# A two-layer attention and MLP kernel on one Trainium2 core: the ramp's loads, score units, bank pairs and query transposes rearranged

## Chip, core and metric

The kernel runs on one core of one Trainium2 chip. The metric is the device time of one launch in microseconds (us). Engines are named as in the profile: PE (TensorE matmul), PEld (its weight load), DVE (VectorE), ACT (ScalarE), POOL (GpSimd), SP (SyncE, which issues DMAs).

## What is computed

A sequence of 2048 tokens of width 576 in bfloat16 passes twice through the same attention block and the same MLP. The inputs `B_x` and the weights are shared by both layers.

```python
def _A_ref(x, wqkv, wo):                    # H = 32 heads, Dh = 18, window W = 256
    qkv = (x @ wqkv).reshape(B, S, 3, H, Dh).transpose(2, 0, 3, 1, 4)
    q, k, v = qkv[0], qkv[1], qkv[2]
    scores = jnp.einsum("bhqd,bhkd->bhqk", q, k) * (Dh ** -0.5)
    mask = (idx[:, None] - idx[None, :] >= 0) & (idx[:, None] - idx[None, :] < W)
    p = softmax(where(mask, scores, -1e9))
    return einsum("bhqk,bhkd->bhqd", p, v).transpose(0, 2, 1, 3).reshape(B, S, D) @ wo
def _B_ref(x, w1, b1, w2, b2):              # F = 4608
    h = gelu(layernorm(x) @ w1 + b1)
    return h @ w2 + b2
x = A_x
for _ in range(2):
    x = x + _A_ref(layernorm(x), A_wqkv, A_wo)
    x = x + _B_ref(layernorm(x), B_w1, B_b1, B_w2, B_b2)
```

## The kernel before

**Tiles and stages.** The tokens are 16 tiles of 128. Four tiles make a chunk, so each layer has four chunks and there are eight in all (`CH`); chunk 0 is the first of layer 1 and chunk 4 the first of layer 2. For each chunk the stages are: layer norm (`ln1`, `ln1_in`), projections q, k, v (`qkv`), scores and exponentials and PV per group of four heads (`E`, `E0`; 8 groups), the output projection with the second layer norm (`tail`), and the MLP in three parts of 12 of its 36 column tiles, first half `G_part` (W1 and gelu), second half `mm2` (W2). The attention of one chunk is laid beside the MLP of the chunk before it, so that ACT's exponentials stand beside PE's MLP matmuls. Chunks 0 and 1 have no earlier MLP to stand beside; the time until the first MLP matmul is called the ramp here.

**How the order is made.** Each operation is a task with a cost, a latency and a priority in `Plan.add`. `Plan.schedule` (line 263) runs a list scheduler over a model of the engines: it takes the task that can start first, ties go by priority, and it gives out the eight PSUM banks with `place` (line 273). The priorities are shifted by a table `PL.nudge`, one number per stage. The resulting order is written out per engine with semaphore waits (`Sched`), and the chip keeps that order on each engine. SP issues all DMAs in one such order; a task on SP that waits holds back all that stand behind it. Where PE would idle in the first 140 us of the plan, filler matmuls are put in (`keep_warm`, `warm_fn`, profile line L683).

**Banks.** Score units take two pairs of banks out of `SC = (0, 2, 4)`, that is banks 0-1, 2-3 or 4-5. Projections, transposes and the MLP's second half take a bank of `FILL`, PV one of `OUT`, both (7, 6, 5, 4). `place` takes among the possible banks the one that has been free longest.

**Start.** SP issues the loads of x tile 0, x tile 1, wq, x tiles 2 and 3, wk, wv (each weight as one large piece and two small ones, `w_load`), then x tiles 4 to 7. The layer norm's statistics are DVE work (L696, L700), the variance step (L709) and the power (L711) POOL work, the normalised tile DVE work (L721). For chunk 0 the normalised tile is transposed on PE (L738) and copied by ACT (L741); later tiles are transposed by DMA (L744). ACT's first instruction is the load of its table for the exponential (L1138).

**Projections.** `qkv` makes q, k and v of a tile with 10 matmuls each (L800 in chunk 0, L781 or L784 in chunk 1, L840 from chunk 2 on). ACT and DVE copy the results (L858, L861, v: L848). k of chunk 0 is transposed on PE (L874) and copied by ACT (L878); q of chunk 0, and all q and k after it, by a DMA transpose from SP (L880).

**Scores.** A score unit is one PE task (L909) of 3 or 4 blocks of 128 query columns for four heads, two exponentials on ACT (L918, 128x768 or 128x1024), and masks on POOL for the blocks at the window's edges (L939). One PV task per group follows (L956), then four DVE steps (L967 to L977). A unit holds one of six slots of the tile `pT` until its PV is done. In the first chunk of a layer there are no keys before it, and each group has three units of 3 blocks: with `(key tile, first query tile, number of query tiles, column)`

```python
if t0 == 0:
    us = [[(0, 0, 3, 0)], [(1, 1, 3, 128)], [(2, 2, 2, 256), (3, 3, 1, 128)]]
```

**Loads in the ramp.** A load may be gated by a name that it reads: wo by `aq0` (chunk 0's first group finished), the first W1 slab by `k3`, the next by `v0h0` and `aq2`, b1 and b2 by `k3`, x tiles 8 to 11 by `v1h0`, tiles 12 to 15 by `xm0_3`, the first W2 third by `aq5` and `aq7`. `xm0_i` is the transposed MLP input of tile i of chunk 0, `xa_i` that of the projections.

Of the kernel before, what the change touches and what calls it, by code (L numbers as in the profile page):

```python
# [9 lines left out]
P = 128  # L10
# [176 lines left out]
class Plan:  # L187
# [75 lines left out]
    def schedule(self):  # L263
# [9 lines left out]
        def place(t):  # L273
# [27 lines left out]
        def starves(t, st, got):  # L301
# [4 lines left out]
            where, when = place(f)  # L306
# [12 lines left out]
        served = {}  # L319
        n = len(self.tasks)  # L320
        while len(order) < n:
            best = None
            cands = []
            for e in ENGS:
                for t in released[e]:
# [4 lines left out]
                    if t.alloc:  # L330
                        got, when = place(t)
# [33 lines left out]
            if t.dma is not None:  # L365
# [15 lines left out]
                done = at + t.move  # L381
                for o in served:
                    if o != t.eng and served[o] > at:
                        both = min(t.move, served[o] - at)
# [3 lines left out]
                q.append((done - t.move, done, t.desc))  # L388
# [42 lines left out]
SWITCH = 0.095  # L431
TURN_FROM = 40.0
# [4 lines left out]
def build_kernel(nc, A_x, A_wqkv, A_wo, B_x, B_w1, B_b1, B_w2, B_b2, out):  # L437
# [19 lines left out]
    PVG = [()] * 8  # L457
# [22 lines left out]
    PL.nudge = {"": -230.72, "b": 275.87, "ea0.0": 68.12, "ea0.2": -36.73, "ea0.p0": 25.27, "ea0.p1": 8.39, "ea0.p2": 19.16,  # L480
# [403 lines left out]
    def units_of(k):  # L884
# [6 lines left out]
        if t0 == 0:  # L891
            us = [[(0, 0, 3, 0)], [(1, 1, 3, 128)], [(2, 2, 2, 256), (3, 3, 1, 128)]]
# [423 lines left out]
```

## Time and profile before

| what | us |
|---|---|
| median of 3 runs (865.04 to 865.78) | 865.6 |
| the profiled execution | 864.13 |
| its span, first to last instruction | 862.3 |
| first projection matmul (L800) begins | 7.56 |
| first MLP matmul (L1076) begins | 87.07 |
| last matmul ends | 859.41 |
| busy time of DVE, ACT, POOL | 392.0, 593.2, 377.9 |

In a line of the timeline, the first number is the start in us from the span's start, the second the length, then engine, line, operation, tile written and tile read with their shapes, and how many instructions are merged in the line; in brackets stands the engine's idle time before it and what ended it. In a line of the groups, the shapes are followed by the count, the busy time and the mean length of one in ns, and the idle time before them. Matmuls overlap in the engine, so the mean length of one is more than what it adds; what it adds is the busy time divided by the count, or the distance to the next instruction.

### The profile page before, as it was taken

The page shows a single profiled execution, that of the slowest core. Times are in us where ns is not written, and L with a number is a line of the kernel's source. Part 1 is how long each engine was busy: PE and PEld are TensorE (multiplying, and loading weights), DVE is VectorE, ACT ScalarE, POOL GpSimd, SP SyncE. Part 2 cuts the span into 40 slices and gives each one's busy share as a digit, 9 for nine tenths or more (in the row PEclk, how much of TensorE's full clock was granted, in tenths as well). Part 3 has the DMA queues.
Part 4 walks back from the last instruction along what each step waited for, and adds up shares of the span by engine and source line. Part 5 has one row for each costly group of instructions (what it writes and reads, how often), then busy time and mean ns, then how long its engine had stood idle before and what let it go on. Part 6 is the DMA issues. An engine that isn't in the chain of part 4 may idle for free.

```text
span 862.3 us, 26990 instructions
## 1 busy us (share of the span) xinstructions
PE 848.7 (98%) x11578; PEld 520.5 (60%) x11578; DVE 392.0 (45%) x934; ACT 593.2 (69%) x741; POOL 377.9 (44%) x560
## 2 busy tenths in 40 slices
PE   8899999999999999999999999999999999999998
PEld 6556556656556565565655655656556656656656
DVE  7689424655228542384424832655224434243012
ACT  4796788768667588573875876737787589771730
POOL 4687544465135653264421863425454276222100
PEclk9999999999999999999999999999999999999999
DMA  7887435351583615957359443673536953355320
GB/s 192 197 193 142 124 125 148 109 163 44 166 181 107 163 43 166 204 93 169 90 151 218 92 139 125 116 177 98 173 112 119 289 155 105 126 166 146 120 83 28
DMA packets 181862, 119.77 MB, mean 139 GB/s; under 512 B 107440, under 2 KB 181744, under 8 KB 181744
## 3 DMA queue, kind: packets, MB, share of 16 engines
q1 hardware_dynamic: 181744, 118.05, 53.7%
q8 instruction: 91, 1.49, 0.7%
q14 instruction: 27, 0.22, 0.1%
HBM read 90.10 MB, written 2.36 MB: 107 GB/s over the span
## 4 chain that ended last, share of the span: by engine, by line
PE 87%; DMA 4%; DVE 4%; ACT 2%; issue 2%; SPq 1%; POOL 1%; POOLq 0%; DVEq 0%; ACTq 0%
PE ps L1076 31%; PE ps L781 27%; PE ps L784 9%; PE ps L840 8%; PE ps L909 6%; PE ps L956 4%; ACT pT L918 2%; DMA xnTm<-xn 2%; PE ps L800 1%; DMA xnTa<-xn 1%; DVE x_res L1019 1%; DVE xn L721 1%; DVE st_all L696 1%; SPq L633 1%; DMA wqkv<-in_A_wqkv_dram 1%
## 5 line engine op out<-in xcount | busy, mean ns | idle before, releaser
L939 POOL TENSOR_SCALAR_AFFINE_SELECT pT<-pT 128x512 bf16<-128x512 bf16 (+1 forms) x368 | 282.8, 789 | 250.1 <-ACT pT L918 244.9
L918 ACT ACTIVATE pT<-ps 128x1024 bf16<-128x1024 f32 (+1 forms) x384 | 345.1, 974 | 58.0 <-PE ps L909 57.6
L1076 PE MATMUL ps<-xnTm,w_sb 64*128 64x512 bf16 x2592 | 290.5, 376 | 0.9 <-DVE x_res L1019 0.3
L1086 ACT ACTIVATE hT<-ps,b1col 128x512 bf16<-128x512 f32 x276 | 167.4, 687 | 173.9 <-PE ps L1076 173.4
L1076 PEld LDWEIGHTS ps<-xnTm,w_sb 64*128 64x128 bf16 x2592 | 128.8, 94 | 142.5 <-issue 6.4
L781 PE MATMUL ps<-w_sb,hT 128*128 128x288 bf16 x1506 | 201.1, 287 | 0.0
L1019 DVE TENSOR_TENSOR x_res<-ps,x_res 128x288 f32<-128x288 f32 x224 | 100.0, 450 | 188.2 <-PE ps L781 162.1
L781 PEld LDWEIGHTS ps<-w_sb,hT 128*128 128x128 bf16 x1506 | 139.9, 98 | 51.5 <-issue 15.6
L840 PE MATMUL ps<-wqkv,xnTa 64*128 64x288 bf16 x1296 | 91.7, 283 | 1.6 <-DVE x_res L1019 1.1
L967 DVE STREAM_TRANSPOSE oq<-ps 128x512 f32<-128x512 f32 x64 | 45.8, 716 | 98.9 <-PE ps L956 98.0
L784 PE MATMUL ps<-w_sb,hT 128*32 128x288 bf16 x2424 | 83.7, 287 | 0.1
L861 DVE CAST qn<-ps 128x288 bf16<-128x288 f32 x120 | 49.0, 450 | 76.4 <-PE ps L840 68.8
L840 PEld LDWEIGHTS ps<-wqkv,xnTa 64*128 64x128 bf16 x1296 | 61.3, 94 | 31.4 <-issue 2.7
L784 PEld LDWEIGHTS ps<-w_sb,hT 128*32 128x32 bf16 x2424 | 62.2, 97 | 13.6 <-issue 4.2
L909 PE MATMUL ps<-qT,kT 32*128 32x384 bf16 (+2 forms) x1216 | 64.1, 276 | 2.8 <-ACT pT L918 2.3
L696 DVE BATCH_NORM_STATS2 st_all<-x_res 128x6 f32<-128x288 f32 (+1 forms) x128 | 53.4, 442 | 6.7 <-DMA x_res<-in_A_x_dram 5.8
L709 POOL TENSOR_SCALAR vtmp<-mv_all 128x1 f32<-128x1 f32 (+1 forms) x43 | 8.8, 204 | 107.7 <-DVE mv_all L700 105.3
L848 DVE CAST vA<-ps 128x288 bf16<-128x288 f32 x64 | 26.5, 450 | 63.2 <-PE ps L840 59.5
L1092 POOL TENSOR_TENSOR x_res<-x_res,b2bc 128x576 f32<-128x576 f32 x32 | 40.2, 1275 | 32.8 <-ACT hT L1086 32.8
L956 PE MATMUL ps<-pT,vA 128*20 128x384 bf16 (+2 forms) x1408 | 50.5, 276 | 0.2 <-DVE qn L861 0.2
L909 PEld LDWEIGHTS ps<-qT,kT 32*128 32x128 bf16 x1216 | 19.4, 92 | 42.8 <-issue 26.3
L781 PE MATMUL ps<-wo_sb,attT 128*128 128x288 bf16 x320 | 42.1, 287 | 0.3 <-DVE qn L861 0.3
(56 smaller groups left out, 465.1 us busy)
## 6 DMA issues: line engine op xcount, KB each, us to landing
w_sb<-in_B_w_dram SPq DMA_DIRECT2D x46, 864.0 KB, 6.0
w_sb<-in_B_w_dram SPq DMA_DIRECT2D x48, 768.0 KB, 4.7
w_sb<-in_B_w_dram SPq DMA_DIRECT2D x96, 48.0 KB, 4.4
wqkv<-in_A_wqkv_dram SPq DMA_DIRECT2D x3, 576.0 KB, 5.6
x_res<-in_A_x_dram SPq DMA_DIRECT2D x3, 576.0 KB, 5.7
wqkv<-in_B_w_dram SPq DMA_DIRECT2D x2, 864.0 KB, 6.3
out_dram<-x_res SPq DMA_DIRECT2D x12, 144.0 KB, 2.0
wo_sb<-in_A_wo_dram SPq DMA_DIRECT2D x4, 144.0 KB, 2.6
```

What stands on the lines that cost most here:

```text
L696: add("dve", lambda e, i=i, s=s: e.bn_stats(st_all[:, t, i, :], s[:, t, i * HB:(i + 1) * HB]), reads=res, writes=[f"st{t}_{i}"], cost=0.37 ...
L781: return e.matmul(bank(b)[:, 0:HB], lhs, rhs, start=start, stop=stop, skip_group_check=True)
L784: ins = e.matmul(bank(b)[32 * j:32 * j + 32, 0:HB], lhs[:, 32 * j:32 * j + 32], rhs, start=start, stop=stop, tile_position=(0, 32 * j), sk ...
L840: ins = e.matmul(bank(bs[o])[:, 0:HB], xnTa[r:r + 64, c, i * 128:(i + 1) * 128], wqkv[r:r + 64, c, col:col + HB], start=(c == 4), stop=(ph ...
L861: add("dve", lambda e, b=bs[o], dst=dst: e.tensor_copy(dst, heads_of(bank(b))), reads=[bs[o]], writes=[f"qn{sl}h{o}"], cost=0.375, lat=0.1 ...
L909: ins = e.matmul(two(bs[j // 2])[:, j % 2, col:col + nq * 128], k_of(T0 + so)[0][32 * j:32 * j + 32, g, :], qs[32 * j:32 * j + 32, g, qo * ...
L918: add("act", lambda e, h2=h2: e.activation(pT[:, sl, 2 * h2:2 * h2 + 2, lo:hi], two(bs[h2])[:, :, lo:hi], ACT.Exp, scale=SCALE), reads=[bs ...
L939: add("pool", lambda e, ap=ap, pat=pat, sgn=sgn, kind=kind: e.affine_select(ap, ap, pattern=pat, compare_op=(ALU.is_ge if kind == "d" else ...
L956: ins = e.matmul(bank(bo)[32 * j:32 * j + VW, qo * 128:(qo + nq) * 128], vA[:, (T0 + so) % VS, 8 * j + g, :], pT[:, sl, j, col:col + nq * ...
L1019: add("dve", lambda e: e.tensor_tensor(x_res[:, t, sl], bank(b)[:, 0:HB], x_old[:, t, sl], ALU.add), reads=[b] + ([f"xin{t}"] if first els ...
L1076: ins = e.matmul(bank(bks[i])[:, 0:n], w1_sb[r:r + 64, sls[i], col:col + 128], xnTm[r:r + 64, k % 2, c, 0:n], start=(c == 4), stop=(ph == ...
L1086: add("act", lambda e, ff=ff, hd=hd, bk=bk: e.activation(hd[:, 0:n], bank(bk)[:, 0:n], ACT.Gelu_apprx_tanh, bias=b1col[:, ff:ff + 1]), rea ...
```

## The change

- **Loads.** x tile 1 and x tiles 2 and 3 are issued from ACT's queue, behind the table load; SP goes from x tile 0 straight to wq, wk, wv. wo is gated by `aq2`; the three first W1 slabs by `aq3`, `aq5` and `xm0_0`; b1 and b2 by `aq5`; x tiles 8 to 11 by `xa2`, 12 to 15 by `aq2` of chunk 1; the first W2 third by `xm0_2` and `xm0_3`.
- **Score units.** In the first chunk of each layer the blocks of a unit may belong to several groups. For groups 0 to 2 of chunk 0 there are 8 units in place of 9; for the other sets of three groups 7 in place of 9, and for the set of two 5 in place of 6. The PV task takes each block from its unit; a slot is given back when the last of its groups is done.
- **Banks.** `SC` gains the pair 6-7. `place` takes the first listed bank of those that are free at the task's start; only where none is does the time count.
- **Queries.** q of tiles 1 and 2 of chunk 0 is transposed on PE, in two halves of four 128x128 transposes with a bank each; ACT copies the first half and DVE the second. q of tiles 0 and 3 stays with the DMA.
- **Layer norm of chunk 0.** The variance step goes from POOL to DVE. For tile 0 the 64 duplicated columns are computed by DVE from x (not copied by ACT), and the five transposes go to two banks, copied by ACT (3) and DVE (2).
- **The planner.** Several modelled costs and latencies of DMAs change, a DMA of 500 descriptors or more behind a transpose gets 0.8 us more (`TURN_DMA`), and the table `PL.nudge` is new throughout, so the order of the tasks is new everywhere.

The diff, cut to its core:

```diff
-                    key = (max(bank_free[b] for b in bs), n)
+                    key = (max(now, max(bank_free[b] for b in bs)), n)
...
-    PL.nudge = {"": -230.72, "b": 275.87, "ea0.0": 68.12, "ea0.2": -36.73, "ea0.p0": 25.27, "ea0.p1": 8.39, "ea0.p2": 19.16,
+    PL.nudge = {"": -0.78, "b": -26.43, "ea0.0": -39.17, "ea0.1": -14.18, "ea0.2": 0.51, "ea0.p0": 239.47, "ea0.p1": -20.24,
...
-    SC = (0, 2, 4)
+    SC = (0, 2, 4, 6)
...
     xin_load(0, 1)
-    xin_load(1, 1)
     w_load(0)
-    xin_load(2, 2)
     w_load(1)
     w_load(2)
+    table("exp", -10)
+    xin_load(1, 1, q="act", prio=-9)
+    xin_load(2, 2, q="act", prio=-8)
...
-        add("pool", lambda e: e.tensor_scalar(vtmp[:, t0:t0 + n], var, sc, bi, op0=ALU.mult, op1=ALU.add),
+        add("dve" if t0 < 4 and not fused else "pool", lambda e: e.tensor_scalar(vtmp[:, t0:t0 + n], var, sc, bi, op0=ALU.mult, op1=ALU.add),
...
+            bs = [Bank(FILL)] * 2 if i else [Bank(FILL), Bank(FILL)]
+            groups = ((0, 1, 2, 3), (4,)) if i else ((0, 1, 2), (3, 4))
...
-                if k == 0 and (w == "k"):
+                if k == 0 and (w == "k" or i in (1, 2)):
+                    n = 2 if w == "q" else 1
+                    for y in range(n):
+                        b = Bank(FILL)
+                        gg = range(y * G // n, (y + 1) * G // n)
...
+                        if y == 0:
+                            add("act", lambda e, dd=dd, src=src: e.copy(dd, src()), reads=[b], writes=[dn], cost=0.12 + 0.83 / n, lat=0.17, prio=prio)
+                        else:
+                            add("dve", lambda e, dd=dd, src=src: e.tensor_copy(dd, src()), reads=[b], writes=[dn + "d"], cost=0.5, lat=0.14, prio=prio)
                     continue
...
-        if t0 == 0:
-            us = [[(0, 0, 3, 0)], [(1, 1, 3, 128)], [(2, 2, 2, 256), (3, 3, 1, 128)]]
...
+        on = lambda g, *ps: [(g,) + p for p in ps]
+        if CH[k][1]:
+            seq = [on(g, *u) for g in gs for u in units_of(k)]
+        elif k == 0 and gs[0] == 0:
+            seq = [on(g, (0, 0, 3, 0)) for g in gs]
+            bs = [on(g, (1, 1, 3, 0), (2, 2, 1, 384)) for g in gs]
+            cs = [on(g, (2, 3, 1, 256 * n), (3, 3, 1, 256 * n + 128)) for g, n in ((0, 0), (1, 1), (2, 0))]
+            seq += [bs[0], cs[0] + cs[1], bs[1], bs[2], cs[2]]
+        else:
+            seq = []
+            for g in gs:
+                seq += [on(g, (0, 0, 3, 0), (2, 2, 1, 384)), on(g, (1, 1, 3, 0), (2, 3, 1, 384))]
+            seq.insert(2, [(g, 3, 3, 1, 128 * n) for n, g in enumerate(gs)])
...
-    xin_load(8, 4, ["v1h0"], -4)
+                xin_load(8, 4, ["xa2"], -4)
...
-                w1_load(-1, ["k3"])
+                w1_load(-1, ["xm0_0"])
-            w2_load(0, 1, ("aq5", "aq7"))
+            w2_load(0, 1, ("xm0_2", "xm0_3"))
...
-                w1_load(-1, ["v0h0"])
-                w1_load(-1, ["aq2"])
+                w1_load(-1, ["aq3"])
+                biases()
+                w1_load(-1, ["aq5"])
...
-                xin_load(12, 4, ["xm0_3"], 0)
+                xin_load(12, 4, ["aq2"], 3)
```

More of the change, by code (lines that the diff above doesn't have):

```diff
@@ L271, in schedule, with place @@
         bank_free = {b: 0.0 for b in range(self.nbanks)}
-        def place(t):
+        def place(t, now):
             got = []
@@ L305, in starves @@
             f = feed[fed]
-            where, when = place(f)
+            where, when = place(f, max(free["pe"], f.ready))
             if where is None:
@@ L801, in fn @@
                 return ins
-            add("pe", fn, reads=reads, writes=[bs[o]], cost=mm_cost(HB) * KD, lat=0.22, prio=prio, alloc=[bs[o]], after=after, mode=mode, wide=wide)
+            add("pe", fn, reads=reads[o] if isinstance(reads[0], list) else reads, writes=[bs[o]], cost=mm_cost(HB) * KD, lat=0.22, prio=prio, alloc=[bs[o]], after=after, mode=mode, wide=wide)
         return bs
@@ L906, in fn @@
             ins = None
-            for (so, qo, nq, col) in parts:
+            for (g, so, qo, nq, col) in tiles:
                 for j in range(4):
@@ L941, in scores, with pv @@
                 reads=[f"p{sl}h0", f"p{sl}h1"], writes=[f"p{sl}m{mi}"], cost=0.12 + 0.475 * nb, prio=prio)
-        return sl
-    def pv(k, g, units, bo, first, last, prio):
-        slots.extend(sl for _, sl in units)
+        return sl, users
+    def pv(k, g, units, prio):
+        bo = Bank(OUT)
+        for _, (sl, users) in units:
+            users.discard(g)
+            if not users:
+                slots.append(sl)
         l, t0, nt = CH[k]
@@ L949, in pv @@
         PL.part = f".p{g}"
+        todo = [(p[1:], sl) for parts, (sl, _) in units for p in parts if p[0] == g]
         def fn(e):
             ins = None
-            todo = [(p, sl) for parts, sl in units for p in parts]
             for n, ((so, qo, nq, col), sl) in enumerate(todo):
@@ L956, in fn @@
                     ins = e.matmul(bank(bo)[32 * j:32 * j + VW, qo * 128:(qo + nq) * 128], vA[:, (T0 + so) % VS, 8 * j + g, :],
-                                   pT[:, sl, j, col:col + nq * 128], start=(first and n == 0), stop=(last and n == len(todo) - 1),
+                                   pT[:, sl, j, col:col + nq * 128], start=(n == 0), stop=(n == len(todo) - 1),
                                    tile_position=(0, 32 * j), skip_group_check=True)
             return ins
-        rd = [f"p{sl}{x}" for _, sl in units for x in ("h0", "h1", "m0", "m1", "m2")]
-        rd += [f"v{(T0 + p[0]) % VS}h{o}" for parts, _ in units for p in parts for o in range(2)]
-        ncol = sum(p[2] for parts, _ in units for p in parts) * 128
+        rd = [f"p{sl}{x}" for _, (sl, _) in units for x in ("h0", "h1", "m0", "m1", "m2")]
+        rd += [f"v{(T0 + p[0]) % VS}h{o}" for p, _ in todo for o in range(2)]
+        ncol = sum(p[2] for p, _ in todo) * 128
         add("pe", fn, reads=rd, writes=[bo], cost=0.02 + ncol * 0.000425, prio=prio, lat=0.2, mode="c",
-            alloc=([bo] if first else ()))
-        if not last:
-            return
+            alloc=[bo])
         add("dve", lambda e: e.transpose(oq[:, 0:4 * nt, :].rearrange("p b c -> p (b c)"), bank(bo)[:, 0:nt * 128]),
@@ L992, in E @@
[L992 to L1009 removed]
+    def E(k, gs, prio):
+        gs = list(gs)
+        on = lambda g, *ps: [(g,) + p for p in ps]
[6 more added lines that the diff above has]
+            seq += [bs[0], cs[0] + cs[1], bs[1], bs[2], cs[2]]
+        else:
+            seq = []
+            for g in gs:
+                seq += [on(g, (0, 0, 3, 0), (2, 2, 1, 384)), on(g, (1, 1, 3, 0), (2, 3, 1, 384))]
+            seq.insert(2, [(g, 3, 3, 1, 128 * n) for n, g in enumerate(gs)])
+        at = {g: max(n for n, u in enumerate(seq) if any(p[0] == g for p in u)) for g in gs}
+        done = []
+        todo = list(gs)
+        for n, u in enumerate(seq):
+            done.append((u, scores(k, u, prio)))
+            while todo and at[todo[0]] + PVLAG <= n:
+                pv(k, todo[0], [x for x in done if any(p[0] == todo[0] for p in x[0])], prio - 0.1)
+                todo.pop(0)
+        for g in todo:
+            pv(k, g, [x for x in done if any(p[0] == g for p in x[0])], prio - 0.1)
@@ L1134, in mm2 @@
         PL.part = ""
-    def table(name, prio):
-        if name == "exp":
-            fn = lambda e: e.preload_act_table_set("exp_and_others")
-        else:
-            fn = lambda e: e.preload_act_table(ACT.Gelu_apprx_tanh)
-        add("act", fn, cost=1.4, lat=0.0, fifo="act", plain=True, prio=prio)
     def ln1(k, prio):
```

147 lines of the change are left out of this document (69 added, 78 removed), and 141 rows, old and new, of the table add.

## The prediction

> **What bounds the kernel now.** I read the busy times of the whole span first, then the same by stage, then TensorE's waits, and the timelines of the stage that loses most. The profiled execution took 864.13 us, with a span of 862.3, so 1.83 us lie around the span; the median shown is 865.6, 1.47 above this execution. Every saving below is worked out in the profiled execution and then taken off the median.
>
> ```profile
> PE 848.7 (98%) x11578; PEld 520.5 (60%) x11578; DVE 392.0 (45%) x934; ACT 593.2 (69%) x741; POOL 377.9 (44%) x560
> ```
>
> TensorE (PE) is the bound. The stage table gives, for each stretch, its length, the busy time of PE, weight load, VectorE (DVE), ScalarE (ACT) and GpSimd (POOL), then the granted clock, the DMA share and GB/s.
>
> ```profile
> 10.29:28.79 18.50, 18.32 (x173) 13.47 (x174) 13.16 (x39) 13.79 (x24) 7.53 (x15) 1.00 0.92 192
> 28.79:36.00 7.21, 4.49 (x81) 2.46 (x79) 3.92 (x14) 3.48 (x6) 4.73 (x7) 0.76 0.92 181
> 36.00:60.00 24.00, 22.58 (x360) 12.95 (x358) 19.64 (x46) 23.78 (x33) 19.00 (x28) 1.00 0.72 156
> 60.00:87.07 27.07, 25.94 (x402) 16.27 (x403) 25.14 (x62) 19.30 (x22) 20.00 (x34) 1.00 0.82 168
> 87.07:860.00 772.93, 770.07 (x10516) 470.23 (x10516) 324.11 (x759) 529.70 (x655) 321.00 (x458) 1.00 0.51 134
> ```
>
> From 87.07 on, PE idles 2.9 us in 773, with 0.6 of it after its last matmul: little can be won there except work. Before, PE idles 0.2, 2.7, 1.4 and 1.1 us in the four stages. The worst, 28.79 to 36, also has a granted clock of 0.76. PE's timeline of it:
>
> ```profile
> 29.46 0.35 PE L909 MATMUL ps<-qT,kT 32*128 32x256 bf16 x8 [0.38 <-DVE mv_all L700]
> 30.72 0.34 PE L909 MATMUL ps<-qT,kT 32*128 32x384 bf16 x4 [0.91 <-ACT pT L918]
> 32.48 2.59 PE L784 MATMUL ps<-wqkv,xnTa 128*32 128x288 bf16 x40 [1.42 <-DMA xnTa<-xn]
> ```
>
> PE waits 0.91 for an exponential and 1.42 for the transposed input of the second chunk. Then its 40 matmuls take 2.59 us; by the row of this form over the span (L784 on hT: 2424 in 83.7 us) they take 1.38, so 1.21 more is lost to the low clock behind the wait. The chain of waits shows what came late:
>
> ```profile
> 22.36 4.98 DMA qT<-qn
> 27.34 0.05 issue
> 27.39 0.31 PE ps L909
> 27.70 4.74 DMA xnTa<-xn
> 32.44 0.04 issue
> 32.48 2.59 PE ps L784 x40
> ```
>
> The transposes of q's fourth tile and of the second xnTa tile land 4.7 to 5.0 us after issue. The SyncE queue shows why they start late: weight and bias loads stand among them (19.41 w1, 19.89 input rows 8 to 11, 21.66 b1, 25.77 b2), and the first xnTa transpose goes out at 23.70, though the last copy it and its three fellows need (POOL L729) ended at 20.49. ACT pays as well:
>
> ```profile
> 29.85 2.92 ACT L918 ACTIVATE pT<-ps 128x768 bf16<-128x768 f32 x4 [0.56 <-PE ps L909]
> 35.95 23.16 ACT L918 ACTIVATE pT<-ps 128x768 bf16<-128x768 f32 x32 [3.18 <-PE ps L909]
> ```
>
> It idles 3.18 us and then runs 23.16 us without a gap, PE stopping for it in bits of 0.20 to 0.34.
>
> **The change part by part.**
>
> Start. PE's second group of L800 begins at 10.29, on the key weights, which land at 10.16. Their first piece is issued at 4.05 and would go out some 1.1 us earlier, with the loads of x1 and x2-3 (0.43 and 0.59 us of issue) gone to ACT, which idles to 5.55 except for its table load. But the DMA share is 0.8 to 1.0 from about 4 us on, and bytes decide: x0 to x3, wq and wk, 1.9 MB, come in any case. If all of them still come first, only the start of the stream moves, 0.43 or less; if the x loads came behind wk, 0.44 MB at the 350 GB/s of this stretch is 1.2 us; if they take half of wq's rate, wq lands up to 0.7 later than 7.5, which the 0.84 us of idle between q's first tile and 10.29 absorbs nearly. Bounds -1.2 and +0.7; I take -0.3, nearest the byte count. The Trainium skill (DMA: Bandwidth & Descriptors, Issuing engines are not separate DMA queues) says that DMAs started from several engines interleave on the same 16 DMA engines and that only issue time is saved; by that the -1.2 falls out. No DMA from ACT is in this trace.
>
> Moving the variance step to DVE and splitting xnTa0's copy over two banks shorten the chain of x0 by a few tenths (POOL L709 0.19 us). It is ready at 6.81 while wq comes at 7.5, so I cost both at nothing. If wq came first, they gain up to 0.5.
>
> q1 and q2 on PE. Two DMA transposes leave SyncE (1.24 us of issue each) and 16 transposes come to PE. L874's row: 8 have a mean of 219 ns, but the next matmul follows after 0.45 us, so 16 cost +0.9, on a PE that is 99% busy there. All in line at 219 ns it would be 3.5. The Trainium skill (TensorE: Matmul & The Clock Gate, Part 4: PE-mode transpose) gives about 275 ns in one kernel and says that the full clock does not engage for transposes; 16 would then cost 4.4 us and the sum below would be near zero. Here the rows show 56 ns from one to the next and a clock of 1.00. The copies, half on ACT (a whole one, L878, is 1.03, so about 1.1 us for two halves) and half on DVE (between the 0.45 of a cast and the 0.72 of L967 each), lie beside a PE-bound stage in which ACT idles 4.7 and DVE 5.3 us. Without that cover, 1.1 us of exponentials would be late.
>
> Later loads. w1, rows 8 to 11, b1 and b2 leave the stretch 19 to 32; SyncE keeps q0, q3 and the xnTa transposes. The first can go at about 20.5 instead of 23.70, four at 1.25 us, with q3's among them: second tile issued by about 24, landing by 29 even at 5 us, when PE gets through chunk 0's projections (28.3 plus 0.9). So the 1.42 wait and the 1.32 us of low clock (1.21, and 0.11 on the 16 matmuls of L956 behind it) go, and of the other 1.3 us I take 0.5: -3.2 in all, bounds 0 and -4.0. What is late next is POOL: the mask that releases the first PV ended at 32.53. The later homes have room: W1 is wanted at 87.07, the second W1 slab group at 117, w2 at 99.8; a w2 load gated by the last two transposes of chunk 0 (before 87) has over 10 us where it takes 5 to 6. If that cover were gone, PE would wait for w2 at once.
>
> Shared units. Chunk 0 has 24 score units of 384 columns and gets 20 (8, 7 and 5); the first chunk of layer 2 gets 19. Columns stay (72 blocks each). The two exponential forms price a unit:
>
> ```profile
> L918 ACT ACTIVATE pT<-ps 128x1024 bf16<-128x1024 f32 x288 | 273.9, 1027 | 42.3 <-PE ps L909 42.0
> L918 ACT ACTIVATE pT<-ps 128x768 bf16<-128x768 f32 x96 | 71.3, 816 | 15.7 <-PE ps L909 15.6
> ```
>
> 0.951 and 0.743 us of busy time each, 0.81 ns a column, so a fixed 0.12: 8 fewer save ACT 0.95 us in chunk 0. Of the 1.42 us that PE idles under that bound I take half: -0.7 (bounds 0, -1.4). On PE a unit of 384 columns takes 0.27 to the next instruction and one of 512 takes 0.33, so 0.09 is fixed: 4 and 5 units, less up to 0.01 for each piece that is cut in two, give -0.3 and -0.4. Masks cost POOL some 0.4 us more (18 singles of 0.62 for 12 and 3 doubles of 1.10), and POOL idles 5 us of those 24.
>
> 60 to 87, and all after. DVE is 93% busy there; I take 0, between -1.5 (PE's idle time with 0.39 of warm-up filler) and +1.5. The new order moves everything behind 87; the idle time in it is bits of 0.2 to 1.1, and I take 0, within 1.6 both ways. A fourth bank pair is for planned order only, and costs nothing by itself; it is costed with the second rival.
>
> Sum: -0.3 + 0.9 - 3.2 - 0.7 - 0.3 - 0.4 = -4.0, so 861.6.
>
> **Rivals.** First, DVE becomes the bound of 60 to 87: what is won before 60 is waited for there. For it speak the 25.14 of 27.07; against it DVE's 13 us of idle time between 20 and 87, and PV results that come earlier too. Left are -0.4 in layer 2 and some 0.6: 864.6.
>
> Second, slower: the planner now takes the first-listed bank of those free at that moment, no longer the one free longest, so a PSUM bank is reused right behind its reader, and any lateness makes PE wait. The price is a stop as in 36 to 60, 0.20 us (L909 on ACT). Some 680 PE tasks after 87 take banks (155 score units, 144 and 192 of the MLP's two halves, 72 projections, 56 each of PV and wo); from 20 stops on, one in 34, the gain is gone, and at one in 15 it is 45 x 0.20 = +9: 870.6. Against it: those places show hardly any stop now, with latencies already in the plan.
>
> Third, the loads are moved, but the transposes land as late as now, since they load the DMA engines themselves: then 2.2 of the 3.2 go, 863.8. Fourth, transposes in line at 219 ns: +2.6, 864.2.
>
> **How the numbers follow.** Forecast 0.66, first rival 0.11, second 0.12, third 0.09, fourth 0.02. A difference of 0.2% (1.7 us) is about what a measurement of this kernel can tell from none, so faster ends at 863.9: 0.66 plus most of the third, 0.72; same 0.15; slower 0.13. The unknown costs reach to 857.5 (the low bounds together: -1.2 + 0.9 - 4.0 - 1.4 - 0.3 - 0.4 - 1.5, some -8) and, with the first rival and a wait or two, to 866.5; outside lie the second rival and 0.05 below.
>
> **What would show it.** Right: no xnTa wait and a clock of 1.00 around 30, the first MLP matmul (L1076) at 83 to 84 instead of 87.07, 18 exponentials fewer, ACT's gap of 3.18 gone. Wrong: L1076 near 87 with DVE waits ahead of it (first), many short PE waits behind 87 (second), xnTa still landing at 32 (third), L874 groups over 1 us (fourth).

## Result and profile after

The changed kernel takes 868.16 us (median of 15 runs, 865.80 to 870.81), the kernel before 865.04 in the same comparison (15 runs): a ratio of 1.0037, 95% interval 1.0023 to 1.0050, so slower by 3.1 us where 4.0 us less were forecast. The profiled execution took 868.56, its span is 866.7 (before 862.3).

The busy times of the whole span and, below, the stage table with the stretches and columns of before (length, PE, weight load, DVE, ACT, POOL, clock, DMA share, GB/s):

```profile
PE 849.5 (98%) x12061; PEld 522.3 (60%) x12061; DVE 393.4 (45%) x943; ACT 591.6 (68%) x724; POOL 377.6 (44%) x563
```

```profile
10.29:28.79 18.50, 17.93 (x193) 12.91 (x193) 12.45 (x35) 14.95 (x26) 7.40 (x14) 1.00 0.39 71
28.79:36.00 7.21, 6.94 (x190) 4.45 (x178) 5.34 (x16) 6.15 (x7) 5.00 (x9) 1.00 1.03 188
36.00:60.00 24.00, 21.83 (x410) 12.44 (x404) 21.07 (x49) 22.08 (x26) 20.76 (x34) 1.00 0.71 122
60.00:87.07 27.07, 24.68 (x415) 14.64 (x409) 23.92 (x61) 18.77 (x20) 19.67 (x34) 1.00 0.84 153
87.07:860.00 772.93, 766.48 (x10801) 469.43 (x10796) 322.06 (x758) 526.85 (x643) 319.67 (x459) 1.00 0.53 138
```

PE's work hardly changed (+0.8 us); its idle time grew by 3.6. The second stretch is what was forecast: PE is busy 6.94 us of 7.21 (4.49 before) and the clock is 1.00 (0.76). But in the next two PE is idle 2.2 and 2.4 us, where it was 1.4 and 1.1, and behind 87.07 it is idle 6.4 us, where it was 2.9. PE's timeline names the waits:

```profile
29.79 0.79 PE L802 MATMUL ps<-wqkv,xnTa 128*128 128x288 bf16 x5
...
30.83 2.16 PE L805 MATMUL ps<-wqkv,xnTa 128*32 128x288 bf16 x60
...
42.57 0.79 PE L802 MATMUL ps<-wqkv,xnTa 128*128 128x288 bf16 x5 [0.91 <-DVE vA L871]
...
44.14 0.79 PE L802 MATMUL ps<-wqkv,xnTa 128*128 128x288 bf16 x5 [0.46 <-DVE oq L1000]
...
62.27 0.34 PE L938 MATMUL ps<-x_res,xnTm 32*128 32x384 bf16 x4 [1.36 <-issue]
...
63.87 0.19 PE L1217 MATMUL ps<-ident,hT 36*128 36x36 bf16 x1 [0.60 <-DMA hT<-in_B_b_dram]
...
87.81 4.49 PE L1104 MATMUL ps<-xnTm,w_sb 64*128 64x512 bf16 x40 [0.47 <-issue]
...
588.92 0.40 PE L938 MATMUL ps<-qT,kT 32*128 32x384 bf16 x8 [1.49 <-DMA kT<-qn]
...
688.73 0.40 PE L938 MATMUL ps<-qT,kT 32*128 32x384 bf16 x8 [1.96 <-DMA kT<-qn]
```

The second chunk's projections begin at 29.79 and go on at 30.83, both with no wait (before, they began at 28.31 and went on at 32.48, behind 1.42). Then come waits for DVE, for chunk 1's transposed q (62.27; the profile names no releaser, but the transpose issued at 58.02 lands 4.2 us later), for the bias b1, and twice for transposed keys. The first MLP matmul begins at 87.81 (87.07 before). The chain of waits around the last of them:

```profile
675.87 3.44 SPq L911
...
681.72 6.76 DMA kT<-qn
688.48 0.25 issue
688.73 0.40 PE ps L938 x8
```

The key transpose stands on SyncE (SP) behind a query transpose (675.87) and three pieces of a W1 slab (679.41 to 681.66, 2.25 us of issue), and lands 6.76 us after its issue.

### The profile page after: what moved, and what is told of

Its sections match the earlier page's. It is cut to its first block, busy times and chain, and to the rows that moved or that the text cites. A ratio compares the mean times of both kernels' runs of the same rounds, so it can differ in the third digit from the quotient of the medians.

```text
span 866.7 us, 27908 instructions
## 1 busy us (share of the span) xinstructions
PE 849.5 (98%) x12061; PEld 522.3 (60%) x12061; DVE 393.4 (45%) x943; ACT 591.6 (68%) x724; POOL 377.6 (44%) x563
## 4 chain that ended last, share of the span: by engine, by line
PE 88%; DMA 3%; ACT 3%; DVE 2%; issue 2%; SPq 1%; POOL 1%; POOLq 0%; DVEq 0%
PE ps L1104 31%; PE ps L802 27%; PE ps L805 10%; PE ps L863 9%; PE ps L938 6%; PE ps L991 4%; ACT pT L949 2%; DMA kT<-qn 1%; PE ps L821 1%; DMA wqkv<-in_A_wqkv_dram 1%; DMA w_sb<-in_B_w_dram 1%; DVE oq L1000 0%; DVE qn L884 0%; ACT hT L1114 0%; POOL pT L970 0%
## 5 line engine op out<-in xcount | busy, mean ns | idle before, releaser
L970 POOL TENSOR_SCALAR_AFFINE_SELECT pT<-pT 128x512 bf16<-128x512 bf16 (+2 forms) x376 | 283.0, 776 | 279.0 <-ACT pT L949 257.8
L949 ACT ACTIVATE pT<-ps 128x1024 bf16<-128x1024 f32 (+2 forms) x366 | 342.8, 1013 | 56.8 <-PE ps L938 56.5
L802 PE MATMUL ps<-w_sb,hT 128*128 128x288 bf16 x1434 | 192.9, 287 | 0.3 <-DVE qn L884 0.3
L802 PEld LDWEIGHTS ps<-w_sb,hT 128*128 128x128 bf16 x1434 | 132.4, 98 | 51.4 <-issue 17.0
L805 PE MATMUL ps<-w_sb,hT 128*32 128x288 bf16 x2712 | 92.5, 286 | 0.1
L805 PEld LDWEIGHTS ps<-w_sb,hT 128*32 128x32 bf16 x2712 | 70.5, 97 | 14.7 <-issue 4.7
L938 PE MATMUL ps<-qT,kT 32*128 32x128 bf16 (+2 forms) x1280 | 62.5, 270 | 4.2 <-DMA kT<-qn 3.5
L733 DVE TENSOR_SCALAR xn<-x_res,mv_all,rstd 128x576 bf16<-128x576 f32 (+1 forms) x64 | 37.6, 605 | 5.1 <-DMA xnTm<-xn 2.6
L802 PE MATMUL ps<-wo_sb,attT 128*128 128x288 bf16 x300 | 39.5, 286 | 0.1
```

Source lines behind the costliest of these rows:

```text
L802: return e.matmul(bank(b)[:, 0:HB], lhs, rhs, start=start, stop=stop, skip_group_check=True)
L805: ins = e.matmul(bank(b)[32 * j:32 * j + 32, 0:HB], lhs[:, 32 * j:32 * j + 32], rhs, start=start, stop=stop, tile_position=(0, 32 * j), sk ...
L938: ins = e.matmul(two(bs[j // 2])[:, j % 2, col:col + nq * 128], k_of(T0 + so)[0][32 * j:32 * j + 32, g, :], qs[32 * j:32 * j + 32, g, qo * ...
L949: add("act", lambda e, h2=h2: e.activation(pT[:, sl, 2 * h2:2 * h2 + 2, lo:hi], two(bs[h2])[:, :, lo:hi], ACT.Exp, scale=SCALE), reads=[bs ...
L970: add("pool", lambda e, ap=ap, pat=pat, sgn=sgn, kind=kind: e.affine_select(ap, ap, pattern=pat, compare_op=(ALU.is_ge if kind == "d" else ...
```

## Experiments

**How they are read.** Edits that move a task keep the written order of everything else; the numbers in them are places in the plan, not measured times. ACT loads its tables 49 times in the same sequence in every kernel, so these loads are milestones: the third, behind the first third of the first MLP half (100.51 in before), and the last (837.39). The table gives the ratio to the kernel before on the same chip (an estimate over all executions of both, which can differ by some tenths of a us from the distance of the two medians), the first MLP matmul (87.07 in before), and the two milestones less those of before, each from one profiled execution.

Beside the time stands the mean granted clock of each execution. In the profile of before it is 0.998, since the clock is 0.50 from 32 to 35, at the wait of 1.42 and behind it. In the lines, the columns are length, PE, clock, DMA share and GB/s:

```profile
32.00:33.00 1.00, 0.52 (x12) 0.50 1.06 333
33.00:34.00 1.00, 1.00 (x24) 0.50 1.06 352
34.00:35.00 1.00, 1.00 (x24) 0.50 0.90 230
```

Of the 116 executions of before beside the experiments, 70 have a mean of 0.996 or 0.998 and 46 have 1.000; on the chip of e1 to e4 the medians are 864.76 at 0.998 and 863.06 at 1.000. All milestones below are taken from that one profile of before, so they count as won about 1.2 us of low clock (2.59 less 1.41 us for the 40 matmuls) that not every execution of before has.

| run | ratio [95%] | first MLP matmul | third load | last load |
|---|---|---|---|---|
| changed kernel | 1.0037 [1.0023, 1.0050] | 87.81 | +0.74 | +4.42 |
| e7, the same again | 1.0033 [1.0017, 1.0049] | 86.12 | -0.94 | +0.68 |
| e1, keys first | 1.0017 [1.0004, 1.0029] | 85.27 | -1.80 | +0.07 |
| e2, early loads | 1.0046 [1.0029, 1.0064] | 88.32 | +1.25 | +5.46 |
| e3, x rows 8 to 11 early | 1.0025 [1.0013, 1.0038] | 85.56 | -1.50 | +0.21 |
| e5, e1 and e3 | 1.0008 [0.9997, 1.0019] | 85.28 | -1.79 | +0.29 |
| e14, e5 again | 1.0006 [0.9994, 1.0017] | 85.46 | -1.60 | -0.19 |
| e13, e5 with fewer q transposes | 1.0012 [1.0000, 1.0023] | 87.56 | +0.50 | +2.46 |
| e9, e5 with twice as many | 1.0062 [1.0039, 1.0085] | 88.22 | +1.15 | +8.08 |
| e12, e5 with banks spread | 1.0020 [1.0004, 1.0035] | 87.50 | +0.43 | +3.96 |
| e8, e5 with longest-free banks | 1.0093 [1.0076, 1.0110] | 85.52 | -1.54 | +7.26 |
| e11, before with first-listed banks | 1.0036 [1.0021, 1.0051] | 86.97 | -0.09 | +3.15 |
| e10, before with x loads on ACT | 0.9986 [0.9971, 1.0001] | 84.44 | -2.62 | -1.66 |
| e4, before with later loads | 0.9977 [0.9966, 0.9989] | 84.46 | -2.61 | -2.73 |
| e6, e4 and e10 | 0.9965 [0.9952, 0.9979] | 83.93 | -3.14 | -2.72 |

### What the later loads and the start are worth alone: e4, e10, e6

e4, in the order of before:

```diff
+            if t.dma == "w1" and "k3" in t.reads:        # first slab
+                st = 29.90
+            elif t.dma == "b" and "b2" in t.writes:
+                st = 29.91
+            elif t.dma == "w1" and "v0h0" in t.reads:
+                st = 33.00
```

> The kernel before with the later loads alone: two W1 slabs and b2 are issued behind the four transposes of chunk 1's input, all other orders are kept. This is the step of the prediction that weighed most (-3.2, of which about 2.6 are the wait for the second input tile and the low clock behind it). T: the wait of 1.42 at 32.48 and the granted clock of 0.76 go and the time falls by about 2.5 us, if nothing in the queue takes it back. R: the transposes land as late as before without the loads beside them, and the time stays within 0.5 us.

862.26 us against 863.95; by the ratio it is faster by 0.23%, 2.0 us. Its stage table and PE's timeline:

```profile
28.79:36.00 7.21, 5.82 (x105) 3.35 (x103) 5.79 (x18) 6.08 (x9) 5.83 (x8) 1.00 0.86 201
```

```profile
30.36 0.34 PE L919 MATMUL ps<-qT,kT 32*128 32x384 bf16 x4 [0.91 <-ACT pT L928]
30.78 1.41 PE L794 MATMUL ps<-wqkv,xnTa 128*32 128x288 bf16 x40
```

The 0.91 us that PE waits for an exponential stays; the 1.42 for xnTa are gone, and the 40 matmuls behind it take 1.41 us in place of 2.59. The 2.61 us gained by the third milestone are still there at the last. At a clock of 1.000 alone, the medians are 861.38 (9 of 12 executions) and 863.06, so some 1.7 us are won without the clock too. The heaviest step of the prediction holds by itself.

e10 takes x tiles 1 to 3 to ACT's queue in the order of before, e6 does both:

```diff
+            if t.dma == "x" and "xin1" in t.writes:
+                st = 1.50
+                t.eng = "act"
+            elif t.dma == "x" and "xin2" in t.writes:
+                st = 1.51
+                t.eng = "act"
```

> The kernel before with x tile 1 and x tiles 2 and 3 issued from ACT's queue, and nothing else. e6 had this with the later loads and ended G's first part 0.5 us ahead of e4. Theory T: alone it gives nothing or nearly (0 to 0.3), since the second xnTa transpose at 32.4, which SyncE sends out behind the weight loads, sets what follows: second projection group at 9.7 to 9.9 in place of 10.29, wait for xnTa at 32 longer by as much. Rival: the start is passed on (0.5 us faster to the end).

> The kernel before with the later loads of e4, and besides x tile 1 and x tiles 2 and 3 issued from ACT's queue. In the changed kernel the second group of projections began 0.6 us earlier with these loads on ACT. If the start is passed on through the ramp: first MLP matmul at 83.8 to 84.2 (84.46 in e4) and 0.3 to 0.6 under e4's time. Rival: the ramp behind 30 is bound by ACT's exponentials and the transposes on SyncE, so the gain at the start is waited for there: level with e4 within 0.3. If bytes decide the order of landing, wq comes later than 7.4 and the time is 0.3 to 0.7 above e4.

e10: 862.49 against 863.48, by the ratio 1.2 us less with an interval from 2.5 less to none, which excludes neither expectation. In its trace the second group of projections begins at 8.95 (10.29 before), with no wait for the key weights:

```profile
8.95 2.61 PE L810 MATMUL ps<-wqkv,xnTa 128*128 128x288 bf16 x20
```

What follows is earlier by about as much: SP sends the first xnTa transpose at 22.53 (23.70 before), PE waits 0.87 for the second in place of 1.42, and the clock behind that wait stays at 1.00. A part of the gain is this clock: 3 of 12 executions of e10 have a mean under 1.000, of before on that chip 10 of 23, and at 1.000 alone the medians are 862.40 and 862.72, only 0.3 us apart.

e6: 861.50 against 864.37, by the ratio 3.0 us less (1.8 to 4.1), and it beats both kernels. That the two savings add is not shown: the interval holds e4's 2.0 as well as the sum, and at the last load e6 and e4 are level.

### What the new order costs: e1, e2, e3, e5, e7, e14

e1 sends out three transposes (one k of layer 2's third chunk, one q and one k of its last) ahead of other SP work, and a W2 piece behind them:

```diff
+            if t.dma == "t" and t.stage == "q6.3" and "k1" in t.writes:
+                st = 577.45
+            elif t.dma == "t" and t.stage == "q7.3" and "q3" in t.writes:
+                st = 673.60
+            elif t.dma == "t" and t.stage == "q7.3" and "k5" in t.writes:
+                st = 673.61
+            elif t.dma == "w2" and "w2x0" in t.writes:
+                st = 675.93
```

> The changed kernel with one thing moved, the order of SyncE's queue in two places of layer 2: the transposes of k's fourth tile of chunks 6 and 7 (and q's of chunk 7) go ahead of transposes and weight loads that are wanted later. Every other engine keeps its order. Theory T (the transposes stand too far back in SyncE's queue, PE reaches their readers first): the two waits of L938 on the k transposes, 1.49 at 588.92 and 1.96 at 688.73, vanish and about 3.4 us go, so the time is level with the kernel before, within 1 us. Rival R (the new order's engine work and bank use set the time, the wait is only where it shows): the waits move to other instructions and the time stays 3 us above before.

865.72 against 863.95, +0.17% (changed kernel +0.37%). Its trace has neither wait for kT; a 0.97 at 575.91 (for a copy of DVE) and a 0.19 at 685.82 stand near. The time lies between the two theories: the waits are gone, and some 1.5 us over before are left. Its ramp has the order of the changed kernel, and yet the waits of 0.91, 0.46, 1.36 and 0.60 between 42 and 64 are not in it (0.54 for DVE and 0.45 for ACT stand between 42 and 45). With the changed kernel and e7, three executions of one ramp order reach the third load at +0.74, -0.94 and -1.80.

e2 issues both biases, wo and a W1 slab ungated into SP's gap at 18:

```diff
+            if t.dma == "b":            # b1, b2
+                st = 17.90
...
+            elif t.dma == "wo":
+                st = 17.92
...
+            elif t.stage == "le0+" and "aq3" in t.reads:
+                st = 17.93
```

> The changed kernel with b1, b2, wo and the first W1 slab issued in the stretch from 17.8 to 24.4 us in which SyncE's queue is empty, without their gates; all other orders are kept. T: PE's wait for b1 (0.60 at 63.87) goes, the last transposes of chunk 1's q and k no longer stand behind eleven loads, so the 1.36 before the scores at 62.27 goes too; the first MLP matmul starts near 86 in place of 87.81, and the time falls by 1 to 2 us. R: the 36 to 87 stretch is bound by DVE and PE work, so the start of the MLP stays within 0.4 of 87.8. Against both: if the loads still run at 24.4 they delay the transposes of chunk 1's input, and PE waits at 30 again as in the kernel before.

869.04, no better than the changed kernel. Both waits at 62 go, and one comes back that the change had removed:

```profile
31.85 0.79 PE L818 MATMUL ps<-wqkv,xnTa 128*128 128x288 bf16 x5 [2.20 <-DMA xnTa<-xn]
```

6.3 us of loads go out from 17.78 to 24.20, and the first two transposes of xnTa behind them land 7.0 and 5.5 us after issue (the first two in the changed kernel after 2.6 and 3.3), 2.20 us too late for PE. That is the old collision again, which the expectation had named as its third case.

e3 loads x rows 8 to 11 at 18 and puts their twelve statistics into DVE's gaps from 25 to 30, where the changed order has them between 32.4 and 37.5:

```diff
+            if t.dma == "x" and "xin8" in t.writes:
+                st = 17.89
+            elif t.eng == "dve" and t.stage == "ln2" and "st8_0" in t.writes:
+                st = 24.9
...
```

> The changed kernel with the load of x tiles 8 to 11 issued at 17.9 (SyncE empty) in place of 27.7, and DVE's statistics of these tiles (12 instructions) put into its gaps between 24 and 30 in place of 32 to 37.7; POOL's power for them is moved up by 3 us. All else keeps its order. T: DVE is relieved where it is busiest, the waits of 0.91 and 0.46 at 42.57 and 44.14 shrink and the MLP starts 0.5 to 1.4 us earlier. R: the start of the MLP stays at 87.8, since the transposes in front of 62.27 and b1 set it whatever DVE does before.

866.31, +0.25%. DVE's busy time from 36 to 60 is 19.85 in place of 21.07, and of the two waits for DVE one of 0.39 is left. The MLP starts 2.2 us earlier than in the changed kernel, but so it does in e1, where nothing in the ramp was moved. By itself this can't be told from the changed kernel (0.12% apart, intervals of 0.13% each); both moves together can:

> The changed kernel with two moves at once and nothing else: the k transposes of tiles q6.3 and q7.3 ahead of other SyncE work (as in e1), and the load of x rows 8 to 11 with its statistics early (as in e3). Theory T (the loss sits in the new order: k transposes queued behind other transfers, 3.5 us of PE waits in the changed kernel's profile, and loads and statistics of chunk 2 put into the dense stretch 28 to 60): the two moves add up only in part, since both runs so far had no long k wait in their profiles; 864.5 to 865.5 where the kernel before has 864, no wait over 0.5 us for kT behind 87, first MLP matmul at 84 to 85.5. Left over and not touched by either move are waits of 0.7 (about 100), 1.0 (about 576) and some 0.3s. Rival R (the new parts themselves cost it: 1.1 us of query transposes, more matmuls in the narrow column mode, bank choice): no better than e1 and e3, 866.

> e5 once more, unchanged, beside e13 on one chip: 1.0008 against the kernel before in its first run, with e12 (the same ramp) at 1.0020. Theory T: the first MLP matmul comes between 85 and 87.5 according to when the last transposes of the MLP's input land (2.6 to 4.5 us after issue so far), and the time is 0 to 2 us above the kernel before, with the waits of 0.74, 0.23, 0.23 and 0.32 behind 87 again. If the waits behind 87 are themselves chance, these differ by over 0.1 us.

e5 takes 864.64 against 864.37 and e14 865.00 against 865.02: level with the kernel before, 0.29% (2.5 us) under the changed kernel (by the two intervals, 0.12 to 0.46%). What is left in e5 behind 87 are waits like this one:

```profile
98.18 0.83 PE L1034 MATMUL ps<-pT,vA 128*20 128x384 bf16 x24 [0.74 <-ACT hT L1157]
```

with 0.23 at 115 and 489, 0.32 at 538, 0.31 at 732; e14, e7 and the changed kernel have the same five to a hundredth. They belong to the order, 1.8 us in all; only the last has a like in before (0.30 at 731). Besides, e5 has 0.37 at 188, 0.27 at 586 and 0.74 at 686, and e14 0.25 at 184, 0.34 at 586 and 0.19 at 686; these differ from execution to execution. From the third milestone to the last, e5 and e14 lose 2.1 and 1.4 us against before.

A part of what the two moves give is the clock. One of the 24 executions of e5 and e14 has a mean under 1.000, but 10 of the 25 of the changed kernel and e7, and 16 of 23 of before on the chip of e5. At 1.000 alone, the medians there are 863.43 (before), 864.60 (e5) and 865.95 (e7): without the low clock, e5 is 1.2 us behind before and not level. At which waits the changed kernel loses its clock is not shown, as both of its profiles have 1.000.

> The changed kernel once more, unchanged, to see what differs from execution to execution in one and the same order, and to have it beside e5 on one chip. Theory T: the waits for kT (3.5 us in the first profile, at 588 and 688) and for b1 and the last transposes of chunk 1 (2.0 us around 62) depend on when transposes land, and so come out differently: each of them between 0 and 2 us, their sum 1 to 5 us; the median 2 to 4 us above the kernel before. Rival R: the waits are fixed by the order and come again within 0.3 us each.

867.05 against 864.37. The order is the same, the waits are not: kT costs 0.27 (at 587.22) and nothing at 688, where it was 1.49 and 1.96; in the first case a wait of 1.05 for a copy at 576.55 stands in its place.

```profile
576.55 0.79 PE L863 MATMUL ps<-wqkv,xnTa 64*128 64x288 bf16 x10 [1.05 <-DVE qn L884]
...
587.22 0.40 PE L938 MATMUL ps<-qT,kT 32*128 32x384 bf16 x8 [0.27 <-DMA kT<-qn]
```

The waits at 62 are smaller too, 0.16 and 0.30 for 1.36 and 0.60; the two for DVE (0.91 and 0.46) come again:

```profile
61.16 0.34 PE L938 MATMUL ps<-x_res,xnTm 32*128 32x384 bf16 x4 [0.16 <-issue]
...
62.46 0.19 PE L1217 MATMUL ps<-ident,hT 36*128 36x36 bf16 x1 [0.30 <-DMA hT<-in_B_b_dram]
```

So the 3.45 us of the first profile are partly chance, theory T is right in kind (its four waits sum to 0.7 us, less than its 1 to 5), and e1's gain can't be put down to them alone. The wait at 688 came in two (the changed kernel, e2) of the four executions with the changed order there; those two also ended the ramp latest. Why is open.

### The query transposes: e9, e13

```diff
-                            for c in gg:
+                            for c in (list(gg) + list(gg) if len(gg) < G else gg):    # e9
+                            for c in (list(gg)[:1] if len(gg) < G else gg):           # e13
```

> e5 with the 16 query transposes on TensorE done twice (the second pass writes the same values into the same banks): a doubled cost. In the changed kernel's profile the 16 take 1.06 us. Theory T (they stand on the path that sets the end of the ramp, as PE was full there): the first MLP matmul comes 0.9 to 1.1 us later than in e5 (85.28) and the time is 0.9 to 1.1 above e5's. Rival: behind 30 the ramp is bound by ACT and by the transposes on SyncE, so PE's extra work is absorbed before 87: first MLP matmul within 0.3 of e5's, time within 0.4.

> e5 with 4 in place of the 16 query transposes on TensorE (each half transposes only its first four heads; the copies keep their size and place and read these 128 columns four times, so queries of tiles 1 and 2 are not the reference's): the cost taken away without a new order. 12 fewer at 56 to 66 ns are 0.7 to 0.8 us of PE. e9 added 1.06 us of the same work at the same place, and its time rose by 4.6 us. Theory T (PE's work at 16 is on the path to 87, about one for one; e9's excess came from an execution with late transposes): 0.5 to 1.0 us under e5 on the same chip. Rival A (it is amplified, since the later order is out of step with the transfers): 2 us or more under e5. Rival B (hidden in the ramp behind 30): within 0.3.

e9: 869.21, +0.62%, so 0.54% (4.6 us) over e5 for 0.89 us of added work (32 transposes end after 1.95 us, 16 after 1.06), far over both expectations. Its profile shows besides it waits of 1.22 before the first MLP matmul, 1.04 for xnTa at 192, and 1.19 and 1.65 before scores at 208 and 691, none of which e5 or e14 has at that length, and a clock of 0.50 from 693 to 695, behind the last of them. How much of these is chance of the execution and how much follows from the later ramp stays open; the median of 6 runs has both.

e13: 865.78, +0.12%, not under e14 (+0.06% on the same chip). Twelve transposes are gone, but the place takes as long: from the first of them to the next projection 1.18 us pass (15.96 to 17.14), in e5 1.19 (15.47 to 16.66). One of the four left waits 0.27 for ACT's copy, and 0.30 pass before the projection:

```profile
16.61 0.23 PE L943 MATMUL ps<-ident,qn 128*128 128x128 bf16 x1 [0.27 <-ACT qn L924]
17.14 0.77 PE L864 MATMUL ps<-wqkv,xnTa 128*128 128x288 bf16 x5 [0.30 <-issue]
```

So of the three answers the rival B fits downward (by the two intervals, e13 is 0.9 us less to 1.9 us more than e14): fewer transposes alone would not have saved the change. The copies on ACT and DVE, which belong to the move of the queries as well, stayed in e13, so what the whole move costs is not shown. Upward there is no cover.

### The bank rule: e8, e11, e12

In a fixed order, each bank use behind 88 is given a bank anew: e8 (on e5) the longest free, e11 (on before) the first listed that is free at the planned start, e12 (on e5) all chosen at once for the widest distance from reader to next use.

```diff
+                key = (max([o.free for ...] + [0.0]), n)     # e8
+                key = (max([o.free for ...] + [st]), n)      # e11
+        for h, c in zip(seen.values(), BANKS):               # e12: a table
+            h.no = int(c)
```

> e5's order, with the PSUM banks behind 88 chosen anew by the rule of the kernel before (the bank that has been free longest, among those that the order leaves open; the order itself and the bank pairs' number stay). The second rival of the prediction (the first-listed rule puts a bank's next use right behind its reader, so PE stops often) expects 2 us or more under e5. Theory T expects no difference over 0.5 us: the trace of the changed kernel has only three or four waits of that kind behind 87 (0.74, 0.23, 0.23 us), of which the 0.74 has no other bank free.

> The kernel before, its order untouched, with the PSUM banks behind 88 chosen anew by the changed kernel's rule (the first listed bank of those that are free at the task's planned start). The second rival of the prediction alone: it expected stops of 0.20 us at one task in 15, up to 9 us. e8 showed that banks badly chosen in a fixed order cost 7 us by waits of 0.3 to 0.6 on the gelu's reader. Theory T (the rule by itself is not what cost the changed kernel its gain, whose trace has five such stops, 1.2 us in all): 0 to +2.5 us over the kernel before. The rival: +3 us or more.

> e5's order, with the banks behind 88 chosen for the whole stretch at once, so that as few uses as possible follow close behind the bank's reader: 130 of 1189 bank uses change, and of 1322 reuses those planned within 1 us of the reader go from 611 to 541 (the kernel before has 486, e11 549). e8's choice had 50 with nothing between (here 16), e11 showed 3 us for a worse choice in the order before. If the first-listed rule is what still costs the changed kernel its 2 us behind 87 (second rival), this comes out 1.5 us or more under e5's ratio of 1.0008, that is at 0.999 or less. Theory T (the order itself leaves no better banks: the 0.74 us wait has none other, and the rest are waits for copies and transposes): within 0.0007 of 1.0008 on both sides, and the waits of 0.74, 0.23, 0.23 and 0.32 come again.

e8: 872.41, 0.85% over e5, which neither theory expected. In the summary of PE's waits (us in total, times, longest), the largest are score matmuls that wait for a gelu to empty their banks:

```profile
PE ps L1006 <- ACT hT L1182: 3.7, 7, 0.6
```

e11: 867.26 against 863.48, +0.36%, a loss as large as the changed kernel's (1.8 to 4.4 us; theory T said at most 2.5, the rival 3 or more). Its stops are fewer and longer than the prediction's 0.20:

```profile
217.06 2.33 PE L1101 MATMUL ps<-xnTm,w_sb 64*128 64x512 bf16 x20 [0.44 <-DVE x_res L1044]
...
326.25 11.83 PE L1101 MATMUL ps<-xnTm,w_sb 64*128 64x512 bf16 x108 [0.46 <-ACT pT L943]
```

e12: 866.39 against 864.90, +0.20%, no gain on e5, with the waits of 0.74, 0.23, 0.23 and 0.32 again. So a bad bank choice costs 3 to 7 us in an order that was not made for it, but the one other choice tried for the changed order gained nothing. That the 0.74 has no other bank is not shown: in e8 it is gone, and a 0.49 for a gelu before scores at 97.85 stands in its place.

## Why the prediction was wrong, point by point

- **Later loads (-3.2).** Right as a mechanism: wait and low clock went, and alone (e4) they give 2.0 us by the times, 2.6 in the profile. The step that failed is "The later homes have room". It looked at when the moved loads are wanted, and not at what stands behind them on SP and DVE. wo, W1 and b1 go out from 46 to 64 in front of and among chunk 1's last transposes, and PE waits at 62: 1.36 and 0.60 us in the changed kernel, 0.16 and 0.30 in e7, under 0.2 each in e1. The statistics of rows 8 to 11 moved with their load and fill DVE from 36 to 60 (21.07 us busy, 19.64 before); PE waits 0.91 and 0.46 there, 0.54 in e1, and 0.39 with the statistics moved away (e3). So the third load comes at +0.74, -0.94 and -1.80 in three executions of this order, where the sum had -3.6; which of these waits took how much of it stays open.
- **Shared units (-0.7, -0.3, -0.4).** The work went: 366 exponentials for 384, 2.3 us of ACT; the score matmuls, all groups summed, take 74.8 us for 76.4. PE's stops for exponentials from 36 to 60 went from five (1.14 us) to one of 0.22. The stretch got no shorter, as DVE was late next (0.91 and 0.46 us): the first rival's mechanism, one stage earlier than I put it.
- **Query transposes (+0.9).** The profile shows 1.1 (L900 3.5 us for 2.4). The Trainium skill (TensorE: Matmul & The Clock Gate, Part 4: PE-mode transpose) gives some 275 ns each and no full clock; here one takes 219 ns on average, 16 end after 1.06 us at a granted clock of 1.00, and the measurement decides.
- **Start (-0.3).** Too small in the traces: the second group of projections begins 1.34 us earlier in e10 (8.95 for 10.29) and 0.63 in the changed kernel (9.66), so "bytes decide" failed and the issue time counted. In the time it is not settled: e10 gains 1.2 us (2.5 to none), and at a clock of 1.000 alone 0.3. The Trainium skill (DMA: Bandwidth & Descriptors, Issuing engines are not separate DMA queues) says that only issue time is saved; the 1.0 us of issue saved here (0.43 and 0.59) lies between the 0.63 and the 1.34 us of the traces.
- **60 to 87 (0, within 1.5).** With the wait at 62, PE's busy time is 1.3 us less than before in the same stretch, inside the bound.
- **After 87 (0, within 1.6).** The worst miss, and the second step that failed. From the third milestone to the last the profile lost 3.7 us (e7: 1.6; e5 and e14, with two moves undone: 2.1 and 1.4). 1.5 us of it are the four stops of the new order that before has not; the rest differs between executions (the waits for kT are 3.45 us in the first profile and 0.27 in e7). The bound came from the 2.9 us that PE idled there, and idle time bounds only what can be won; nothing bounds what a new order can lose.
- **Rivals.** The second named the right sign, but not for its reason: stops for banks are 1.2 us in the changed kernel's trace (0.74, 0.23, 0.23), 1.8 if the 0.32 and 0.31 behind DVE's copies count too, and not 45 times 0.20. That its rule can cost as much in another order (e11) doesn't show that it did here. The third and fourth didn't come.

The account, from the forecast of -4.0 to the measured +3.1: 2.5 us are undone by the two moves of e5; 1.8 to 2.0 us are what the ramps of e5 and e14 are short of the 3.6 forecast for it (third milestone -1.8 and -1.6); 1.8 to 2.5 us are what e5 and e14 lose behind it, with the 0.4 forecast there. Some 0.3 to 0.8 stay unexplained, within what executions of one order differ. The sizes are measured; that the waits named above are the causes of the middle two parts is in part argued, since they are read from single executions.

## What to carry to other kernels

A load that is moved out of one crowd joins another: ask not only when its data are wanted, but which transfers it is put in front of on its queue, and price those. Where a planner writes the whole order anew, a part that is worth 3 us alone can be lost in it; put the part into the old order first (e6, 3.0 us faster) and let idle time bound gains only, never losses. Read the granted clock of every execution before a difference of medians is put down to a wait.

## What the runs showed of the hardware

The landing time of one and the same transpose differs between executions. Four transposes feed the first MLP matmul; the tile view of them, and PE's timeline, in e12 and in e5, whose ramps are the same instructions:

```profile
DMA to landing us min/median/max: 2.6/3.1/4.5
```

```profile
87.50 4.71 PE L1169 MATMUL ps<-xnTm,w_sb 64*128 64x512 bf16 x42 [2.02 <-issue]
```

```profile
DMA to landing us min/median/max: 2.6/2.7/3.5
```

```profile
85.28 4.92 PE L1147 MATMUL ps<-xnTm,w_sb 64*128 64x512 bf16 x44 [0.44 <-issue]
```

The last of the four, issued at 82.7 and 82.2, lands after 4.5 us in e12 and after 2.6 in e5, and PE waits 2.02 and 0.44 us. A single profile can thus be 1.6 us off at 87 by one landing, which is over a third of what this change was forecast to bring; the same order has to be profiled twice before a wait of that kind is put down to it.
